# Attention and MLP interleaved on one core: bursts of up to four score chunks between whole FFN2 groups

## The chip, the cores and the metric

The kernel runs on one core of one Trainium2 chip. The metric is the device time of one execution in microseconds (us); less is better. The core has a matrix engine (PE, with PEld for its weight loads), a vector engine (DVE), a scalar engine (ACT), GpSimd (POOL) and a queue engine (SP) that issues DMAs. Matmul results go to PSUM, which has eight banks; DVE and ACT read them from there and write to SBUF.

## The reference

Two layers follow each other. For each of 8 batches and 12 heads, with 448 positions of 64 features:

```
scores = (1/8) * q @ k.T
attn   = max(scores, 0)**2 / 448
out    = attn @ v                       # heads side by side: x, 3584 x 768
h      = x @ w_in                       # 768 -> 2048
g      = max(h, 0) + alpha * min(h, 0)  # alpha per column
result = g @ w_out                      # 2048 -> 768
```

Inputs and output are float32; the kernel multiplies in bf16 and accumulates in float32.

## The kernel before

**Units of work.** Four heads of one batch are a quad; there are 24 quads, three for each batch. A quad has seven score chunks (j = 0 to 6, `scores`, line 150) and one A@V (`attnv`, line 189). A chunk is four matmuls on 64x64 quarters of PE, two for each of two PSUM banks (its halves, r = 0 and 1). Relu turns a chunk in PSUM into a bf16 tile `rl`: with "act" ACT does both halves in one instruction (line 173), with "act2" in two (line 169), with "both" ACT does half 0 and DVE half 1 (lines 165 and 166). `squares` (line 176) then lets DVE square `rl` into `at` (line 184). A@V is 28 quarter matmuls into two banks, which ACT copies, scaled, to `xT` (line 217).

The MLP of a batch is 16 FFN1 steps (`ffn1`, line 224: six matmuls of 448 columns on the whole array into one bank, called hps; ACT makes `neg` at line 238, DVE makes `gT` at line 239) and FFN2 groups (`ffn2`, line 242). A group is 16 matmuls of 384 columns that accumulate in one bank, called ops, and that DVE copies to `osb` (line 255); every second group is followed by two stores on SP. One call of `ffn2` is half a group, 8 matmuls. Batches go in pairs: after the FFN1 of an even batch six groups are ready, after that of an odd batch eight.

**PSUM.** The pool `scps` has two buffers of two banks for chunks and A@V. The pool `mmps` has four buffers of one bank, shared by hps, ops, and by the chunks that are called with `space=mm_ps` (their two halves are two buffers named sch).

**Order.** Everything is written out by hand, and each engine executes its instructions in the order of the program. From batch 1 on, a list `stream` holds the chunks of quads 6 to 23, with the A@V of a quad two chunks into the next quad (line 438). It is cut into bursts of three units after a first one of two (line 441), 49 in all. `spread` (line 314) puts them between the steps of the MLP: in the FFN1 part of a batch two or three, in its FFN2 part five to seven, placed by a share of summed costs, so that a burst may stand between the two halves of a group. In a burst (`group`, line 288) the scores come first and A@V last; of three units, the first chunk uses `mmps`. Then come the squares, and for the chunk with j = 0 the SP work of later quads: `load` of q, k, v of quad n + 2 (line 91), and DMA transposes of k and q of quad n + 1 (line 128). With j = 4, POOL casts q, k and v of quad n + 2 to bf16 (line 109). The DMA queue of SP works in order.

Batch 0 and the first six quads stand in a part of their own ahead of this loop, and the FFN of batch 7 follows after it.

Of the kernel before, what the change touches and what calls it, by code (L numbers as in the profile page):

```python
# [24 lines left out]
def kernel(  # L25
# [10 lines left out]
    nc = tc.nc  # L36
    B, H, S, D = q.shape
    d_model, d_ff = moe_w_in.shape
    assert H * D == d_model and S == PP * NJ and D == 64 and H % 4 == 0
    NG = H // 4  # L40
# [7 lines left out]
    def pool(name, bufs, **kw):  # L48
        return ctx.enter_context(tc.tile_pool(name=name, bufs=bufs, **kw))
# [5 lines left out]
    v_pool = pool("vp", 4)  # L55
    early_pool = pool("early", 2)
    qkT_pool = pool("qkT", 2)
    rl_pool = pool("rl", 3)
    at_pool = pool("at", 10)
    xT_pool = pool("xT", 2)  # L60
    g_pool = pool("g", 2)
    neg_pool = pool("neg", 3)
    o_pool = pool("o", 3)
    sc_ps = pool("scps", 2, **PSUM)
    mm_ps = pool("mmps", 4, **PSUM)
# [39 lines left out]
    def copy(eng, o, i):  # L105
        if eng is nc.scalar:
            nc.scalar.copy(o, i)
        else:
            eng.tensor_copy(o, i)  # L109

    def to_bf16(n, w, eng):
        r = raw.pop((n, w))
        if w == "v":
            t = v_pool.tile([128, 2, NJ, D], BF16, tag="v", name="vb")
            vb[n] = t
            copy(eng, t, r)
        else:
            t = cast_pool.tile([128, NJ, 2, D], BF16, tag=w, name=f"{w}b")
            cast[(n, w)] = t
            copy(eng, t.rearrange("p j s d -> p s j d"), r)  # L120
# [29 lines left out]
    def scores(n, j, relu="act", space=sc_ps):  # L150

        if space is mm_ps:
            half = [mm_ps.tile([128, 512], F32, tag="mm", name="sch") for _ in range(2)]
        else:
            ps = sc_ps.tile([128, 2, 512], F32, tag="sc", name="sc")
            half = [ps[:, r] for r in range(2)]
        for r in range(2):
            for c in range(2):
                nc.tensor.matmul(half[r][64 * c:64 * c + 64, :S],  # L159
                                 kT[n][64 * r:64 * r + 64, j, c, :],  # L160
                                 qT[n][64 * r:64 * r + 64, :, c, :],
                                 start=True, stop=True)
        rl = rl_pool.tile([128, 2, S], BF16, tag="rl", name="rl")
        if relu == "both":
            nc.scalar.activation(rl[:, 0], half[0][:, :S], ACTF.Relu)  # L165
            nc.vector.tensor_scalar(rl[:, 1], half[1][:, :S], 0.0, None, ALU.max)  # L166
        elif relu == "act2":
            for r in range(2):
                nc.scalar.activation(rl[:, r], half[r][:, :S], ACTF.Relu)  # L169
        elif relu == "dve":  # L170
            nc.vector.tensor_scalar(rl, ps[:, :, :S], 0.0, None, ALU.max)
        else:
            nc.scalar.activation(rl, ps[:, :, :S], ACTF.Relu)  # L173
        todo.append((n, j, rl))

    def squares(keep=0, both=False):
        while len(todo) > keep:
            n, j, rl = todo.pop(0)
            a = at_pool.tile([128, 2, S], BF16, tag="at", name="at")
            if both:  # L180
                nc.scalar.activation(a[:, 0], rl[:, 0], ACTF.Square)
                nc.vector.tensor_tensor(a[:, 1], rl[:, 1], rl[:, 1], ALU.mult)
            else:
                nc.vector.tensor_tensor(a, rl, rl, ALU.mult)  # L184
            att[(n, j)] = a
# [38 lines left out]
    def ffn1(b, ff, kms=range(KM)):  # L224
        if b % 2 == 0 and ff == 0 and kms[0] == 0:
            gT[b // 2] = g_pool.tile([128, KF, 2 * S], BF16, tag="g", name="gT")
        if kms[0] == 0:
            hps[ff] = mm_ps.tile([128, S], F32, tag="mm", name="hps")
        ps = hps[ff]
        for km in kms:  # L230
            nc.tensor.matmul(ps, w_in_sb[:, km // 2, km % 2, bass.ts(ff, 128)],  # L231
                             xT[b][:, km // 2, km % 2, :],
                             start=(km == 0), stop=(km == KM - 1))
        if kms[-1] != KM - 1:
            return

        neg = neg_pool.tile([128, S], F32, tag="neg", name="neg")
        nc.scalar.activation(neg, ps, ACTF.Relu, scale=-1.0)  # L238
        nc.vector.scalar_tensor_tensor(gT[b // 2][:, ff, (b % 2) * S:(b % 2) * S + S],  # L239
                                       neg, beta_sb[:, ff:ff + 1], ps, ALU.mult, ALU.add)  # L240

    def ffn2(sb, c, hf, half):
        if half == 0:
            ops[(sb, c, hf)] = mm_ps.tile([128, 384], F32, tag="mm", name="ops")
        ps = ops[(sb, c, hf)]
        for ff in range(8 * half, 8 * half + 8):
            nc.tensor.matmul(ps, gT[sb][:, ff, bass.ts(c, 128)],  # L247
                             w_out_sb[:, ff, bass.ts(hf, 384)],
                             start=(ff == 0), stop=(ff == KF - 1))
        if half == 0:  # L250
            return
        if (sb, c) not in o_sb:
            o_sb[(sb, c)] = o_pool.tile([128, d_model], F32, tag="o", name="osb")
        o = o_sb[(sb, c)]
        nc.vector.tensor_copy(o[:, bass.ts(hf, 384)], ps)  # L255
        if hf == 1:
            for u in range(2):
                blk = 2 * c + u
                b, j = 2 * sb + blk // NJ, blk % NJ
                rows = out[b * S:(b + 1) * S].rearrange("(pp j) d -> j pp d", j=NJ)  # L260
                nc.sync.dma_start(out=rows[j], in_=o[64 * u:64 * u + 64])
# [18 lines left out]
    def steps(b, what):  # L280
        if what == "in":
            return [(1.12, lambda ff=ff: ffn1(b, ff)) for ff in range(KF)]
        cs = range(0, 3) if b % 2 == 0 else range(3, 7)
        return [(1.3, lambda c=c, hf=hf, h=h: ffn2(b // 2, c, hf, h)) for c in cs for hf in range(2) for h in range(2)]


    NQ = len(quads)
    def group(units, how="both"):

        def f():  # L290
            order = sorted(units, key=lambda u: u[1] == "av")
            for i, (n, j) in enumerate(order):
                if j == "av":
                    attnv(n)
                elif i == 0 and len(order) == 3:
                    scores(n, j, how, mm_ps)
                else:
                    scores(n, j)
            squares()
            for n, j in order:  # L300
                if n < n_pe:
                    continue
                if j == 0:
                    if n + 2 < NQ:
                        load(n + 2)
                    if n + 1 < NQ:
                        transpose(n + 1, "k")
                        transpose(n + 1, "q")
                if j == 4 and n > 2 * NG and n + 2 < NQ:
                    for w in "kqv":  # L310
                        to_bf16(n + 2, w, nc.gpsimd)
        return f

    def spread(seq, items, share=0.92):

        total = sum(x[0] for x in seq) * share
        done, n = 0.0, 0
        for cost, fn in seq:
            while n < len(items) and done >= total * n / len(items):
                items[n]()  # L320
                n += 1
            fn()
            done += cost
        assert n == len(items)
# [83 lines left out]
    def g(*units):  # L408
        return group([(int(u[0]), "av" if u[1:] == "a" else int(u[1:])) for u in units])
# [24 lines left out]
    stream = []  # L434
    for n in range(2 * NG, NQ):
        for j in range(NJ):
            stream.append((n, j))
            if j == 1 and n > 2 * NG:
                stream.append((n - 1, "av"))
    stream.append((NQ - 1, "av"))  # L440
    parts = [stream[:2]] + [stream[i:i + 3] for i in range(2, len(stream), 3)]

    count = 0
    for b in range(1, B - 1):
        n_in, n_out = ((2, 7 if b == 1 else 6) if b % 2 else (3, 5))
        if b == B - 2:
            n_out = len(parts) - count - n_in
        mlp = steps(b, "in")
        bursts = [group(x, "act2") for x in parts[count:count + n_in]]
        if b == 1:  # L450
            bursts.append(lambda: [to_bf16(2 * NG + 2, w, nc.gpsimd) for w in "kqv"])
        spread(mlp[3:] if b == 1 else mlp, bursts, 0.95)
        count += n_in
        spread(steps(b, "out"), [group(x) for x in parts[count:count + n_out]], 0.92)
        count += n_out
    for _, fn in steps(B - 1, "in") + steps(B - 1, "out")[:-4]:
        fn()
    ffn2_last(B // 2 - 1, NJ - 1)
# [30 lines left out]
```

## Time and profile before

| what | value |
|---|---|
| median of 8 runs | 398.59 us (397.36 to 399.82) |
| the profiled execution | 398.51 us |
| its span, first to last instruction | 396.7 us |
| granted PE clock, mean | 0.991 |
| DVE busy | 256.3 us (65%) |
| ACT busy | 220.8 us (56%) |
| POOL busy | 70.7 us (18%) |
| PE, FFN1 matmuls (line 231) | 768, 150.7 us |
| PE, FFN2 matmuls (line 247) | 864, 147.9 us |

The span is 1.8 us shorter than the profiled execution's own time; a change of the span is a change of the time. The busy time of PE is built from modelled ends of matmuls that overlap, so what an interval on PE costs is better read from where the rows start. A wait on PE that is shorter than a matmul's modelled length does not show as idle time.

### The profile page before, as it was taken

Reading aid. Unit: us, or ns where it says so; the run is one execution under the profiler, and the core shown is the slowest. Engines: PE = TensorE matmul, PEld = TensorE weight load, DVE = VectorE, ACT = ScalarE, POOL = GpSimd, SP = SyncE. Lnnn points to the kernel's source line nnn. Section 1 sums busy time; section 2 is a strip of 40 time slices with the busy share of each in tenths; the row PEclk is TensorE's granted clock in tenths of the full one; section 3 lists DMA queues with packets and bytes.
Section 4 is the critical chain, followed back from the end, with each engine's and each line's share of the span. In section 5 each row is a group of like instructions: output and inputs, shape, how many; then the busy total and the mean of one; then the engine's idle time right before and its main releaser. Section 6 shows DMA issues by size and latency. Waiting matters only on the chain.

```text
span 396.7 us, 7988 instructions
## 1 busy us (share of the span) xinstructions
PE 386.2 (97%) x3217; PEld 202.2 (51%) x3217; DVE 256.3 (65%) x416; ACT 220.8 (56%) x347; POOL 70.7 (18%) x88
## 2 busy tenths in 40 slices
PE   8788999999999999999999999999999999999996
PEld 5434455445555445544555455554555545555564
DVE  3775866677685767577665787768676676636421
ACT  5785856676465766456544675556454575524300
POOL 6664000022030250032010360033002300000000
PEclk9699999999999999999999999999999999999999
DMA  6999997493498963393088971296048820120033
GB/s 140 187 208 204 204 226 255 96 271 100 102 198 189 215 190 80 85 276 97 2 210 183 244 222 23 67 263 186 2 126 183 224 49 0 41 64 17 0 81 80
DMA packets 64485, 55.45 MB, mean 140 GB/s; under 512 B 35760, under 2 KB 60224, under 8 KB 64448
## 3 DMA queue, kind: packets, MB, share of 16 engines
q1 hardware_dynamic: 53232, 44.78, 44.7%
q0 software_dynamic: 10976, 9.96, 15.8%
q8 instruction: 25, 0.41, 0.4%
q10 hardware_dynamic: 240, 0.20, 0.2%
q14 instruction: 12, 0.10, 0.1%
HBM read 45.62 MB, written 11.01 MB: 143 GB/s over the span
## 4 chain that ended last, share of the span: by engine, by line
PE 91%; DMA 6%; ACT 1%; issue 0%; DVE 0%; ACTq 0%; POOLq 0%
PE ops L247 36%; PE hps L231 36%; PE av L202 7%; PE sc L159 4%; PE sch L159 4%; DMA ke<-in_k_dram 3%; DMA w_in_sb<-in_moe_w_in_dram 2%; DMA vb<-in_v_dram 2%; PE ops L270 1%; PE warm L336 1%; PE tps L134 1%; ACT rl L173 0%; ACT xT L217 0%; DVE osb L272 0%; DVE warm_x L330 0%
## 5 line engine op out<-in xcount | busy, mean ns | idle before, releaser
L231 PE MATMUL hps<-xT,w_in_sb 128*128 128x448 bf16 x768 | 150.7, 353 | 1.3 <-ACT xT L211 0.5
L247 PE MATMUL ops<-w_out_sb,gT 128*128 128x384 bf16 x864 | 147.9, 327 | 0.0
L184 DVE TENSOR_TENSOR at<-rl 128x896 bf16<-128x896 bf16 x167 | 109.7, 678 | 19.7 <-ACT rl L173 8.8
L247 PEld LDWEIGHTS <-gT 128*128 128x128 bf16 x864 | 81.1, 98 | 64.9 <-issue 14.2
L231 PEld LDWEIGHTS <-w_in_sb 128*128 128x128 bf16 x768 | 73.3, 98 | 75.2 <-issue 9.5
L239 DVE SCALAR_TENSOR_TENSOR gT<-neg,beta_sb,hps 128x448 bf16<-128x448 f32 x128 | 84.0, 677 | 36.6 <-ACT neg L238 36.4
L238 ACT ACTIVATE neg<-hps 128x448 f32<-128x448 f32 x128 | 68.5, 553 | 56.8 <-PE hps L231 56.0
L173 ACT ACTIVATE rl<-sc 128x896 bf16<-128x896 f32 x109 | 95.4, 926 | 2.1 <-PE sc L159 1.8
L255 DVE COPY osb<-ops 128x384 f32<-128x384 f32 x54 | 30.0, 555 | 51.5 <-PE ops L247 51.5
L165 ACT ACTIVATE rl<-sch 128x448 bf16<-128x448 f32 x44 | 23.9, 544 | 60.7 <-PE sch L159 60.7
L109 POOL CAST kb<-kraw 128x896 bf16<-128x896 f32 x16 | 15.1, 943 | 210.4 <-DMA kraw<-in_k_dram 210.4
L166 DVE TENSOR_SCALAR rl<-sch 128x448 bf16<-128x448 f32 x44 | 27.3, 621 | 15.2 <-PE sch L159 15.2
L159 PE MATMUL sc<-qT,kT 64*64 64x448 bf16 x440 | 34.3, 360 | 2.9 <-ACT rl L173 2.2
L202 PE MATMUL av<-at,vb 64*64 64x448 bf16 x616 | 33.1, 350 | 0.0
L159 PEld LDWEIGHTS <-kT 64*64 64x64 bf16 x672 | 14.9, 106 | 28.7 <-issue 23.8
L202 PEld LDWEIGHTS <-vb 64*64 64x64 bf16 x672 | 20.3, 110 | 13.3 <-issue 1.4
L217 ACT ACTIVATE xT<-av 128x896 bf16<-128x896 f32 x21 | 19.4, 922 | 7.4 <-PE av L202 7.3
L169 ACT ACTIVATE rl<-sch 128x448 bf16<-128x448 f32 x28 | 13.7, 543 | 16.9 <-PE sch L159 16.9
L159 PE MATMUL sch<-qT,kT 64*64 64x448 bf16 x232 | 22.6, 379 | 0.0
L109 POOL CAST qb<-qraw 128x896 bf16<-128x896 f32 x16 | 17.2, 1078 | 0.0
L109 POOL CAST vb<-vraw 128x896 bf16<-128x896 f32 x16 | 16.7, 1044 | 1.0 <-DMA vraw<-in_v_dram 0.9
L144 POOL DMA_DIRECT2D w_in_sb<-in_moe_w_in_dram x12 | 7.6, 636 | 4.6 <-DMA vb<-in_v_dram 2.1
(52 smaller groups left out, 75.5 us busy)
## 6 DMA issues: line engine op xcount, KB each, us to landing
out_dram<-osb SPq DMA_DIRECT2D x54, 192.0 KB, 2.8
qraw<-in_q_dram SPq DMA_DIRECT2D x19, 448.0 KB, 4.7
kraw<-in_k_dram SPq DMA_DIRECT2D x19, 448.0 KB, 5.3
vraw<-in_v_dram SPq DMA_DIRECT2D x18, 448.0 KB, 6.3
w_out_sb<-in_moe_w_out_dram POOLq DMA_DIRECT2D x2, 1536.0 KB, 20.8
w_in_sb<-in_moe_w_in_dram POOLq DMA_DIRECT2D x8, 192.0 KB, 8.0
w_in_sb<-in_moe_w_in_dram POOLq DMA_DIRECT2D x4, 384.0 KB, 9.7
vb<-in_v_dram POOLq DMA_DIRECT2D x6, 224.0 KB, 10.1
```

The lines of the kernel that those rows point to most:

```text
L109: eng.tensor_copy(o, i)
L159: nc.tensor.matmul(half[r][64 * c:64 * c + 64, :S], kT[n][64 * r:64 * r + 64, j, c, :], qT[n][64 * r:64 * r + 64, :, c, :], start=True, st ...
L165: nc.scalar.activation(rl[:, 0], half[0][:, :S], ACTF.Relu)
L166: nc.vector.tensor_scalar(rl[:, 1], half[1][:, :S], 0.0, None, ALU.max)
L173: nc.scalar.activation(rl, ps[:, :, :S], ACTF.Relu)
L184: nc.vector.tensor_tensor(a, rl, rl, ALU.mult)
L202: nc.tensor.matmul(half[r][64 * s:64 * s + 64, :S], vb[n][64 * r:64 * r + 64, s, j, :], a[64 * r:64 * r + 64, s], start=(j == 0), stop=(j ...
L231: nc.tensor.matmul(ps, w_in_sb[:, km // 2, km % 2, bass.ts(ff, 128)], xT[b][:, km // 2, km % 2, :], start=(km == 0), stop=(km == KM - 1))
L238: nc.scalar.activation(neg, ps, ACTF.Relu, scale=-1.0)
L239: nc.vector.scalar_tensor_tensor(gT[b // 2][:, ff, (b % 2) * S:(b % 2) * S + S], neg, beta_sb[:, ff:ff + 1], ps, ALU.mult, ALU.add)
L247: nc.tensor.matmul(ps, gT[sb][:, ff, bass.ts(c, 128)], w_out_sb[:, ff, bass.ts(hf, 384)], start=(ff == 0), stop=(ff == KF - 1))
L255: nc.vector.tensor_copy(o[:, bass.ts(hf, 384)], ps)
```

## The change

The FFN2 part of a batch is no longer handed to `spread`. It is written as whole groups of two `ffn2` calls, and a table says after which group a burst stands and how many units it takes: after groups 0, 2, 3, 4 and 6 of batch 1; 0, 2, 3, 5 and 6 of the other odd batches; 0, 2, 3 and 4 of the even ones. Bursts have four units in 18 of these places and three or fewer in the others. The FFN1 part keeps bursts of three; batch 1 gets one more there. A@V of a quad now follows after three chunks of the next quad instead of two.

In a burst of four the first chunk is on `mmps` with "act2". A second chunk is on `mmps` too, with "both": the last of four chunks, or the third of three chunks that are followed by A@V. Its two banks are the next two that `mmps` hands out.

The pool `rl` goes from 3 to 5 buffers, `at` from 10 to 14, and `gT` from 2 to 1.

```diff
-    rl_pool = pool("rl", 3)
-    at_pool = pool("at", 10)
+    rl_pool = pool("rl", 5)
+    at_pool = pool("at", 14)
...
-    g_pool = pool("g", 2)
+    g_pool = pool("g", 1)
...
-    def group(units, how="both"):
+    def group(units, how=("both", "both")):
...
+            m = len(order)
+            in_mm = {3: [0], 4: [0, 2 if order[-1][1] == "av" else 3]}.get(m, [])
             for i, (n, j) in enumerate(order):
                 if j == "av":
                     attnv(n)
-                elif i == 0 and len(order) == 3:
-                    scores(n, j, how, mm_ps)
+                elif i in in_mm:
+                    scores(n, j, how[in_mm.index(i)], mm_ps)
                 else:
                     scores(n, j)
...
-            if j == 1 and n > 2 * NG:
+            if j == 2 and n > 2 * NG:
                 stream.append((n - 1, "av"))
...
     for b in range(1, B - 1):
...
+            bursts = [group(take(3), ("act2",)) for _ in range(2 if b % 2 else 3)]
+        spread(mlp, bursts, 0.95)
...
+        if b == 1:
+            sizes = {0: 4, 2: 4, 3: 3, 4: 4, 6: 4}
+        elif b == B - 2:
+            sizes = {0: 4, 2: 4, 3: 3, 4: 1}
+        elif b % 2:
+            sizes = {0: 4, 2: 4, 3: 3, 5: 4, 6: 3}
+        else:
+            sizes = {0: 4, 2: 4, 3: 4, 4: 3}
+        mlp = steps(b, "out")
+        for i in range(0, len(mlp), 2):
+            mlp[i][1]()
+            mlp[i + 1][1]()
+            if i // 2 in sizes:
+                group(take(sizes[i // 2]), ("act2", "both") if sizes[i // 2] == 4 else ("both",))()
```

More of the change, by code (lines that the diff above doesn't have):

```diff
@@ L437, with take @@
             stream.append((n, j))
-            if j == 1 and n > 2 * NG:
+            if j == 2 and n > 2 * NG:
                 stream.append((n - 1, "av"))
     stream.append((NQ - 1, "av"))
-    parts = [stream[:2]] + [stream[i:i + 3] for i in range(2, len(stream), 3)]
-    count = 0
+    def take(m):
+        x = stream[:m]
+        del stream[:m]
+        return x
     for b in range(1, B - 1):
-        n_in, n_out = ((2, 7 if b == 1 else 6) if b % 2 else (3, 5))
-        if b == B - 2:
-            n_out = len(parts) - count - n_in
         mlp = steps(b, "in")
-        bursts = [group(x, "act2") for x in parts[count:count + n_in]]
         if b == 1:
[L451 to L455, printed above, removed]
+            bursts = [group(take(2)), group(take(3), ("act2",)),
+                      lambda: [to_bf16(2 * NG + 2, w, nc.gpsimd) for w in "kqv"], group(take(3), ("act2",))]
+            mlp = mlp[3:]
+        else:
[7 more added lines that the diff above has]
+            sizes = {0: 4, 2: 4, 3: 3, 5: 4, 6: 3}
+        else:
+            sizes = {0: 4, 2: 4, 3: 4, 4: 3}
[5 more added lines that the diff above has]
+                group(take(sizes[i // 2]), ("act2", "both") if sizes[i // 2] == 4 else ("both",))()
+    assert not stream
     for _, fn in steps(B - 1, "in") + steps(B - 1, "out")[:-4]:
```

## The prediction

> **What bounds the kernel now.** First the page: busy times, then the slices.
>
> ```profile
> PE 386.2 (97%) x3217; PEld 202.2 (51%) x3217; DVE 256.3 (65%) x416; ACT 220.8 (56%) x347; POOL 70.7 (18%) x88
> ...
> PE   8788999999999999999999999999999999999996
> ```
>
> PE is the bound, and from the third slice on without a visible hole. The list of waits, for PE alone from 79 us to the end, has one entry:
>
> ```profile
> PE hps L231 <- ACT xT L217: 0.2, 1, 0.2
> ```
>
> So PE's time is its matmuls, the cost of switching between MLP and bursts, and stalls too short to show as idle. Next the timeline, PE around 200 to 213 us, with the other engines' rows of the burst at 208 us (start, length; a row is a run of like instructions):
>
> ```profile
> 203.54 0.38 PE L159 MATMUL sch<-qT,kT 64*64 64x448 bf16 x4
> ...
> 208.08 0.38 PE L159 MATMUL sch<-qT,kT 64*64 64x448 bf16 x4
> 208.18 0.56 DVE L255 COPY osb<-ops 128x384 f32<-128x384 f32 x1 [2.18 <-PE ops L247]
> 208.29 0.55 PE L159 MATMUL sc<-qT,kT 64*64 64x448 bf16 x8
> 208.50 0.54 ACT L165 ACTIVATE rl<-sch 128x448 bf16<-128x448 f32 x1 [2.09 <-PE sch L159]
> 208.66 0.61 DVE L166 TENSOR_SCALAR rl<-sch 128x448 bf16<-128x448 f32 x1
> 208.77 4.07 PE L247 MATMUL ops<-w_out_sb,gT 128*128 128x384 bf16 x24
> ...
> 212.78 0.38 PE L159 MATMUL sch<-qT,kT 64*64 64x448 bf16 x4
> ```
>
> For the pure rates I take the unbroken FFN2 at the end, where a copy follows each group, and an A@V in the chain that ended last:
>
> ```profile
> 375.06 0.56 DVE L255 COPY osb<-ops 128x384 f32<-128x384 f32 x1 [1.34 <-PE ops L247]
> 377.66 0.56 DVE L255 COPY osb<-ops 128x384 f32<-128x384 f32 x1 [2.04 <-PE ops L247]
> ```
> ```profile
> 204.12 1.32 PE av L202 x28
> ```
>
> A group of 16 takes 2.60 us, 0.1625 a matmul. Four quarter matmuls run side by side: 1.32 / 7 = 0.19 us for a set, so a chunk is 0.19 and an A@V 1.32.
>
> **1. Fewer bursts.** From the burst at 208.08 to the next at 212.78 are 4.70 us: 24 x 0.1625 = 3.90 for FFN2, 3 x 0.19 = 0.57 for chunks, and 0.23 left. From 203.54 to 208.08: 4.54 - 2.60 - 2 x 0.19 - 1.32 = 0.24. A burst costs about 0.23 us whatever is in it: the change of PE's tiling, in and out. Chunks, A@V and MLP matmuls stay the same in number. The stream of 144 units made 49 bursts; now there are 43 (8 in batch 1, 7 in each of five others). 6 x 0.23 = **-1.4 us**. Cutting a group in two cost nothing beyond its burst, so whole groups gain nothing more.
>
> The Trainium skill ("TensorEngine Tiling (Array Packing)", Key Properties) says that changing the tiling mode drains the array, and "TensorE: Matmul & The Clock Gate" (Step-by-step: what each phase is for) puts a drain at about 128 cycles; at its 2.4 GHz two drains are an estimated 0.11 us a burst. The row says 0.23; by the page the gain would be 0.6 us instead of 1.4, and the sum below 401.2.
>
> **2. The second chunk on `mmps`.** This is what decides. `mmps` has four buffers. Counted in the program's order, after a group come the two halves of the first chunk, then the two of the second such chunk: the last of these four is the bank of the group just finished. The order of the changed program's instructions shows it: in each of the 18 bursts of four this half waits for DVE's copy of the group in front of the burst. In no burst of this loop before did a chunk need that bank.
>
> From the rows at 208, with the burst's first matmul as zero: the copy starts at 0.10 and ends at 0.66 (208.74). A matmul starts some 0.05 after DVE has freed its bank (below: at 175.11, after the first `gT` since 174.39, of 0.67). So the half may start at 0.71. Without a wait the third chunk would start at 0.21 + 0.19 = 0.40, the fourth at 0.59. PE takes its instructions in order, and what follows waits too.
> - Three chunks and A@V: 0.71 - 0.40 = 0.31 us. There are 7: in batch 1 after groups 0 and 6, in batches 3 and 5 after group 0, in batches 2, 4 and 6 after group 2. 7 x 0.31 = 2.2.
> - Four chunks: 0.12 us. The next group takes the bank of the first chunk's half 0, which ACT frees at 0.42 + 0.54 + 0.05 = 1.01, where it would have started at 0.69 + 0.19 = 0.88; so 0.13 in all. 11 x 0.13 = 1.4.
>
> Sum **+3.6 us**. Bounds: nothing, if the wait is hidden in some way that the rows do not show (it can't be a gain: a wait only delays). Above: the copy can start late, if DVE is behind. It is tight where one group alone lies between a burst and one of four: after group 3 of batches 2 and 4, and after group 4 of batch 1. In the first two the burst before (three chunks and A@V) gives DVE a half relu, done about 1.7 us after the burst's start, and three squares of 0.62: 3.6. The next copy is due at 1.83 (from 203.54 to the next `ops` at 205.37) + 0.19 + 0.31 + 2.60 + 0.2 = 5.1. Batch 1 has about as much to spare. Squares can take twice as long next to POOL's casts:
>
> ```profile
> 171.79 0.93 POOL L109 CAST kb<-kraw 128x896 bf16<-128x896 f32 x1 [22.68 <-DMA kraw<-in_k_dram]
> 171.91 2.55 DVE L184 TENSOR_TENSOR at<-rl 128x896 bf16<-128x896 bf16 x2 [0.18 <-ACT rl L173]
> 174.39 2.44 DVE L239 SCALAR_TENSOR_TENSOR gT<-neg,beta_sb,hps 128x448 bf16<-128x448 f32 x4
> 175.11 1.99 PEld L231 LDWEIGHTS <-w_in_sb 128*128 128x128 bf16 x11 [0.28 <-issue]
> ```
>
> Two squares take 2.55 instead of 1.24. Three so slowed add 1.9, which would make the copy some 0.4 to 0.6 late: at three places up to 1.8 us. I take the undisturbed rows, as those casts fall elsewhere.
>
> **3. Two old stalls.** In the rows above FFN1 waits at 175.11 for a bank (0.19 us), as at 316.27 (0.12): squares slowed by casts, right behind a burst. In the changed order the casts there start about as the burst does, and not 2 us into it; the squares are through in time. **-0.3 us**; between -0.3 and, were each stall doubled, +0.3.
>
> **4. What is covered.** In a burst of four with one group behind it, DVE has 0.56 + 0.61 + 4 x 0.62 = 3.65 us and ACT 2 x 0.54 + 2 x 0.93 + 0.54 = 3.5, against 0.1 + 0.88 + 0.13 + 2.60 = 3.7 on PE: the last square waits for ACT's last relu, so the next copy is some 0.45 late, but there a burst of three follows, which does not need that bank. `rl` and `at` only get more buffers; ACT waited 0.3 us once for an `rl`, off PE's path. With one `gT`, the first write of a pair must follow the last read of the pair before; PE has ended that read before it starts the FFN1 step whose result is written, so the wait is over when it is asked: 0.
>
> SP and POOL keep their sequence; what moves is time. A transpose is late when stores and loads stand ahead of it:
>
> ```profile
> 199.18 1.13 SPq L261 DMA_DIRECT2D out_dram<-osb  x2
> 200.37 0.58 SPq L91 DMA_DIRECT2D qraw<-in_q_dram  x1
> 203.61 3.73 SPq L128 DMA_TRANSPOSE qT<-qb  x1
> ```
>
> This `qT` landed at 210.90, 10.5 us after that load's start (in the trace's other such cases 10.5 to 11.2), and was used at 212.78. In batches 3 and 5 of the changed order the same chain runs from the end of group 1: 0.75 for the copy, 1.2 for the stores (199.18 to 200.37), 10.5 to 11.2: landed after 12.5 to 13.2. Its first use is the fourth chunk behind group 5, after four groups (10.4), a burst of four (1.1), one of two chunks and A@V (1.9) and 0.7: 14.1. Covered, with 0.9 to 1.6 us to spare; if that is gone, PE stands still for what is missing, at two places.
>
> **Sum.** 398.5 - 1.4 + 3.6 - 0.3 = **400.4 us**, against this execution's 398.51; the median of the runs is 398.59.
>
> **Rivals.**
> - *The waits do not bite* (0.12): faster. The only loss is the 18 waits, so they decide: the sign turns where their mean falls under 1.7 / 18 = 0.09 us. If the copy ended before the half is due, the result is 398.5 - 1.7 = 396.8. For it: nothing in the profile; against it: the copy begins only 0.10 after the burst and takes 0.56 every time.
> - *Half of it* (0.18): only the A@V bursts pay, and in the others the wait sinks into the change of tiling behind the fourth chunk: 398.5 - 1.7 + 2.2 = 399.0. For it: 0.13 is small against a row; against it: the change of tiling comes after the late half.
> - *DVE or the transposes fall behind* (0.15): 400.4 + 1.8 for three late copies, or + 0.5 to 1 for each late transpose: 401.3 to 402.2.
> - The forecast itself (0.55): 399.9 to 401.0, with the prices of 0.31 and 0.13 give or take 0.03 (18 x 0.03 = 0.5), and step 3 up to its upper end.
>
> A measurement of this kernel tells about 0.3% (1.2 us) from no change. Slower by more: the third, and the forecast but for 0.05 that the spread of the runs takes below 399.7: 0.65. Same: those 0.05, the second, and 0.02 of the first, 0.25. Faster: 0.10. The range leaves out the first rival and the top of the third: 398.2 to 401.9.
>
> **What would show it.** The trace after should have 43 bursts; in each of the 18 of four, the last sch half should start 0.71 us after the burst's first matmul, 0.05 after the copy's end; the chain should pass through `osb` at line 255; the waits at 175 and 316 should be gone. Wrong if that half starts at 0.40 or 0.59, if bursts cost other than 0.23, or if a transpose ends a wait of PE.

## The result, and the profile after

| | before | after |
|---|---|---|
| median | 398.45 us (32 runs, 397.11 to 399.82) | 400.29 us (11 runs, 399.42 to 401.02) |
| the profiled execution | 398.51 us | 400.25 us |
| its span | 396.7 us | 398.5 us |
| time of after / time of before | | 1.0048 [1.0035, 1.0061] |

The change makes the kernel 1.8 us slower, half a per cent. Ratios, here and below, leave out runs more than 1.5% above the fastest of their kernel (two runs of experiment 3); the medians are of all runs. First the page of after: busy times and the chain of work that ended last, by engine.

```profile
PE 387.7 (97%) x3217; PEld 205.1 (51%) x3217; DVE 251.5 (63%) x409; ACT 223.4 (56%) x366; POOL 72.4 (18%) x88
...
PE 90%; DVE 3%; ACT 2%; DMA 2%; issue 1%; POOL 0%; ACTq 0%
```

PE does the same 3217 matmuls and is as full as before. The list of PE's waits from 79 us on is empty: by that view alone nothing is lost. The loss is in the timeline, in waits shorter than a matmul's modelled length. This is after, PE, DVE and ACT around a burst of three chunks and A@V (start, length, engine, line):

```profile
192.83 0.38 PE L159 MATMUL sch<-qT,kT 64*64 64x448 bf16 x4
192.93 0.56 DVE L255 COPY osb<-ops 128x384 f32<-128x384 f32 x1 [1.34 <-PE ops L247]
193.04 0.36 PE L159 MATMUL sc<-qT,kT 64*64 64x448 bf16 x4
193.23 0.69 PE L159 MATMUL sch<-qT,kT 64*64 64x448 bf16 x4
...
193.55 1.69 PE L202 MATMUL av<-at,vb 64*64 64x448 bf16 x28
...
195.18 0.50 PE L247 MATMUL ops<-w_out_sb,gT 128*128 128x384 bf16 x2
```

The first chunk takes 0.38 us as a row, the third 0.69: 0.31 more with the same four matmuls. The copy of the group in front ends at 193.49 (192.93 + 0.56); the third chunk's second half, the late half from here on, starts at 193.55, and A@V right behind it. The same view eight microseconds later, a burst of four chunks:

```profile
200.48 0.38 PE L159 MATMUL sch<-qT,kT 64*64 64x448 bf16 x4
200.59 0.56 DVE L255 COPY osb<-ops 128x384 f32<-128x384 f32 x1 [2.04 <-PE ops L247]
200.70 0.55 PE L159 MATMUL sc<-qT,kT 64*64 64x448 bf16 x8
200.90 0.98 ACT L169 ACTIVATE rl<-sch 128x448 bf16<-128x448 f32 x2 [4.62 <-PE sch L159]
...
201.07 0.50 PE L159 MATMUL sch<-qT,kT 64*64 64x448 bf16 x4
...
201.51 0.66 PE L247 MATMUL ops<-w_out_sb,gT 128*128 128x384 bf16 x3
```

Here the last chunk is 0.50 long, 0.12 more. Taken from the starts of single matmuls, the late half (here that of the last chunk) starts 0.717 to 0.720 us after the burst's first matmul in every one of the 18 bursts of four, 0.05 after the copy's end. Where a burst costs 0.19 for each set of four matmuls and 0.22 besides, the 25 others leave no rest at all (0.00 each); the seven with A@V leave 0.334 each, the eleven of four chunks 0.144: 2.34 + 1.59 = 3.93 us.

**Two parts of the program.** From the first burst of the loop (at about 79 us) to the last matmul of the program, before took 312.87 us in its profile and after 315.61: 2.74 more, where the spans differ by 1.8. The rest is ahead of the loop, in instructions that are the same. In before's one profile the first burst comes at 80.17, in after's at 79.16. The granted PE clock, on the page of before and then on that of after:

```profile
PEclk9699999999999999999999999999999999999999
```
```profile
PEclk9899999999999999999999999999999999999999
```

The second slice is 0.6 in before and 0.8 in after. So before's own execution came to the loop 1.0 us late, after a lower clock. That the clock is the cause is likely, not shown: of the 46 runs of before beside the experiments, the 12 with a granted clock of 0.991 or less, as in this profile, have a median of 398.8 us, the 13 with 0.998 or more 397.8; but experiment 1's profile, with 0.9 in that slice, is no earlier at the loop than after's.

### The profile page after: what moved, and what is told of

Same layout as the page of the kernel before. It is cut to its first block, busy times and chain, and to the rows that moved or that the text cites. A ratio compares the mean times of both kernels' runs of the same rounds, so it can differ in the third digit from the quotient of the medians.

```text
span 398.5 us, 7955 instructions
## 1 busy us (share of the span) xinstructions
PE 387.7 (97%) x3217; PEld 205.1 (51%) x3217; DVE 251.5 (63%) x409; ACT 223.4 (56%) x366; POOL 72.4 (18%) x88
## 4 chain that ended last, share of the span: by engine, by line
PE 90%; DVE 3%; ACT 2%; DMA 2%; issue 1%; POOL 0%; ACTq 0%
PE ops L247 36%; PE hps L231 34%; PE av L202 7%; PE sch L159 6%; PE sc L159 4%; DVE at L184 2%; DMA qe<-in_q_dram 2%; PE ops L270 1%; ACT rl L173 1%; PE tps L134 1%; DMA qraw<-in_q_dram 1%; PE avh L202 1%; DVE gT L239 0%; ACT rl L169 0%; ACT neg L238 0%
## 5 line engine op out<-in xcount | busy, mean ns | idle before, releaser
L173 ACT ACTIVATE rl<-sc 128x896 bf16<-128x896 f32 x97 | 85.1, 930 | 1.8 <-PE sc L159 1.8
L169 ACT ACTIVATE rl<-sch 128x448 bf16<-128x448 f32 x66 | 32.3, 542 | 67.1 <-PE sch L159 67.1
L202 PE MATMUL av<-at,vb 64*64 64x448 bf16 x616 | 34.5, 350 | 0.0
L159 PE MATMUL sc<-qT,kT 64*64 64x448 bf16 x392 | 30.5, 356 | 3.3 <-ACT rl L173 2.2
L159 PEld LDWEIGHTS <-kT 64*64 64x64 bf16 x672 | 17.0, 105 | 32.2 <-issue 26.2
L159 PE MATMUL sch<-qT,kT 64*64 64x448 bf16 x280 | 30.5, 370 | 0.0
L165 ACT ACTIVATE rl<-sch 128x448 bf16<-128x448 f32 x37 | 20.7, 560 | 13.5 <-PE sch L159 13.5
L166 DVE TENSOR_SCALAR rl<-sch 128x448 bf16<-128x448 f32 x37 | 22.9, 620 | 8.4 <-PE sch L159 8.4
L202 PEld LDWEIGHTS <-vb 64*64 64x64 bf16 x672 | 21.4, 109 | 11.7 <-issue 1.4
L109 POOL CAST vb<-vraw 128x896 bf16<-128x896 f32 x16 | 18.0, 1126 | 0.0
```

Source lines behind the costliest of these rows:

```text
L159: nc.tensor.matmul(half[r][64 * c:64 * c + 64, :S], kT[n][64 * r:64 * r + 64, j, c, :], qT[n][64 * r:64 * r + 64, :, c, :], start=True, st ...
L202: nc.tensor.matmul(half[r][64 * s:64 * s + 64, :S], vb[n][64 * r:64 * r + 64, s, j, :], a[64 * r:64 * r + 64, s], start=(j == 0), stop=(j ...
```

## The experiments

Each ratio is against the kernel before on the same chip (its medians there: 398.29 us for experiments 1 to 4, 398.14 for 5 to 7).

**1. The pools alone.** Before, with the three new buffer counts.

```diff
-    rl_pool = pool("rl", 3)
-    at_pool = pool("at", 10)
-    g_pool = pool("g", 2)
+    rl_pool = pool("rl", 5)
+    at_pool = pool("at", 14)
+    g_pool = pool("g", 1)
```

> The kernel before with the buffer counts of the changed one alone (rl 5, at 14, gT 1); order and bursts as before. My theory (bursts gain 1.4 us, the wait for the copy of the group just finished loses 3.9): the pools do nothing, 398.5 us, a ratio of 1.000, and the loop has the same two stalls of FFN1. Rival (the pools do part of it: the changed kernel's profile reached its first burst of the loop 1.0 us earlier than before's): about 397.4, with that burst near 79.2 us in place of 80.2. Second rival (one gT buffer makes DVE wait between pairs of batches): slower than 398.5, with a wait of PE at the start of batches 2, 4 and 6.

398.42 us, ratio 1.0008 [0.9993, 1.0023]: the pools do nothing. With before's order of work, its profile has the loop's first burst at 79.13, so before's 1.0 us there isn't the order's. Its loop takes 313.68, because FFN1 waits five times for a bank, 0.11 to 0.44 us, 1.15 in all, where before's profile had two waits, 0.31 in all. So such waits differ between two profiles with one and the same order of work; whether the buffer counts have a part in that, one profile of each does not tell.

**2. The late half after A@V.** The changed kernel, with A@V ahead of the third chunk in the seven bursts that have both.

```diff
-            in_mm = {3: [0], 4: [0, 2 if order[-1][1] == "av" else 3]}.get(m, [])
+            av_last = order[-1][1] == "av"
+            in_mm = {3: [0], 4: [0, 3]}.get(m, [])
+            if m == 4 and av_last:
+                order = order[:2] + [order[3], order[2]]
```

> The changed kernel with one swap: in the seven bursts of three chunks and A@V, A@V (1.32 us) goes ahead of the third chunk, so that the bank of the group just finished is asked for at 0.40 + 1.32 = 1.7 us after the burst's start, with the copy done at 0.66. Nothing else changes, 43 bursts. My theory: 7 x 0.33 = 2.3 us less, 398.0 us; the eleven bursts of four chunks keep their 0.14. Rival (a second chunk on the shared banks costs by itself, wherever it stands): no change, 400.3.

397.52 us, ratio 0.9987 [0.9972, 1.0002]; after stood at 1.0048, so this edit gives back 0.6%, 2.4 us. Timeline of this kernel, the same burst as above:

```profile
191.22 0.38 PE L159 MATMUL sch<-qT,kT 64*64 64x448 bf16 x4
191.32 0.56 DVE L255 COPY osb<-ops 128x384 f32<-128x384 f32 x1 [1.34 <-PE ops L247]
191.43 0.36 PE L159 MATMUL sc<-qT,kT 64*64 64x448 bf16 x4
...
191.62 1.49 PE L202 MATMUL av<-at,vb 64*64 64x448 bf16 x28
...
192.94 0.36 PE L159 MATMUL sch<-qT,kT 64*64 64x448 bf16 x4
...
193.24 0.34 PE L247 MATMUL ops<-w_out_sb,gT 128*128 128x384 bf16 x1
```

The copy starts 0.10 and ends 0.66 after the burst's start as before, but nobody waits for it: the third chunk comes at 1.72, and takes 0.36. These seven bursts lose 0.01 us together instead of 2.34, with the chunk still on `mmps`: a second chunk there costs nothing by itself. The eleven of four chunks, which have no A@V to put ahead, still lose 0.144 each. The loops of the two profiles differ by 2.73: 2.33 from the seven bursts, and 0.40 because FFN1 waits 0.11 us for a bank here and 0.51 in after.

**3. Bursts of three or fewer.** The changed kernel's whole groups, but 50 bursts, none of four, one after nearly every group.

```diff
-            sizes = {0: 4, 2: 4, 3: 3, 5: 4, 6: 3}
+            sizes = {0: 3, 1: 3, 2: 3, 3: 3, 4: 3, 5: 3, 6: 3}
...
-            sizes = {0: 4, 2: 4, 3: 4, 4: 3}
+            sizes = {0: 3, 1: 3, 2: 3, 3: 3, 4: 3}
```

> The changed kernel with whole groups and all its buffers, but bursts of at most three units: 50 of them, 7 more than in the changed kernel and one more than before, and no second chunk on the shared banks. My theory: 7 x 0.22 = 1.5 us more for bursts, 3.9 us less for the waits: 400.3 - 2.4 = 397.9; measured against before one burst more, 398.5 + 0.2 = 398.7 (the two sums differ by what the profiles' first 80 us differ, 1.0 us, and by 0.2 in FFN1's stalls). Rival (whole groups themselves cost, since all the copies now come right at a burst): 400 or more. Second rival (whole groups gain by themselves): below 397.5.

409.73 us (six runs, 404.91 to 412.94), ratio 1.0244 [1.0202, 1.0286]: about 10 us slower by the ratio, and not the test it was meant to be. The list of PE's waits (total, times, longest) has an entry that neither before nor after has:

```profile
PE sc L159 <- DMA qT<-qb: 7.4, 2, 4.1
```

Timeline of SP's queue and of PE at the first of the two:

```profile
154.49 1.12 SPq L261 DMA_DIRECT2D out_dram<-osb  x2
156.06 0.40 SPq L91 DMA_DIRECT2D qraw<-in_q_dram  x1
...
157.61 1.97 SPq L128 DMA_TRANSPOSE kT<-kb  x1
159.68 3.23 SPq L128 DMA_TRANSPOSE qT<-qb  x1
```
```profile
161.94 0.36 PE L159 MATMUL sc<-qT,kT 64*64 64x448 bf16 x4
165.62 0.38 PE L159 MATMUL sc<-qT,kT 64*64 64x448 bf16 x4 [3.32 <-DMA qT<-qb]
165.93 4.45 PE L247 MATMUL ops<-w_out_sb,gT 128*128 128x384 bf16 x16
```

The transpose stands behind stores, loads and another transpose; its first user starts 11.1 us after the first of them, but the denser bursts ask for it earlier. The stalls cost twice: the group behind the first took 4.38 us (165.93 to 170.31), that behind the second 5.01, against 2.70 elsewhere with its change of tiling, because PE's granted clock fell to 0.83 from 160 to 170 us and 0.66 from 260 to 270. Priced by starts, the two bursts lose 3.5 and 4.5 us and the groups behind them 1.7 and 2.3; with one burst more than before (0.22) that is 12.2 of the 12.3 us by which the loop of this profile is longer than that of before's.

**4. Three chunks in each burst.** 43 bursts, three chunks each but the last; A@V goes into FFN2 bursts ahead of the third chunk, so that the late half always has A@V in front of it. Batch 1 begins with a burst of three instead of two.

```diff
+    def burst(av=False):
+        x = chunks[:3]
+        del chunks[:3]
+        return x + ([(turned.pop(0), "av")] if av else [])
...
+            plan = {0: True, 2: True, 3: False, 4: True}
...
+                units = [(turned.pop(0), "av")] if av is None else burst(av)
+                group(units, ("act2", "both") if av else ("both",))()
```

> A version that keeps the 43 bursts and drops the waits: every burst has three chunks, and three bursts of a batch have A@V besides, all of them in the FFN2 part, with A@V ahead of the third chunk, which alone uses a second pair of the shared banks. My theory: the six bursts less give 1.3 us, no wait is left, FFN1's stalls stay 0.3 to 0.5: 398.5 - 1.3 = 397.2, from 396.8 to 397.6; faster than both. Rival (a second chunk on the shared banks costs by itself; 16 remain): 397.2 + 16 x 0.2 = 400.4. Second rival (fewer bursts gain nothing): 398.5.

396.77 us, ratio 0.9965 [0.9948, 0.9983]: below both kernels. All 18 waits are gone: none of the 17 late halves here has one. A new one of 0.65 us stands at the loop's first burst. Timeline of PE there:

```profile
79.02 0.38 PE L159 MATMUL sch<-qT,kT 64*64 64x448 bf16 x2
...
79.68 0.38 PE L159 MATMUL sch<-qT,kT 64*64 64x448 bf16 x2 [0.28 <-DVE gT L239]
```

A chunk on `mmps` there needs a bank of an FFN1 result that DVE has not yet turned into `gT`; the chunk's second half starts 0.66 after the first.

**5. The copy twice.** After, with a second DVE copy of the group (into a scratch tile) ahead of each of the 18 bursts, to see whether the late half follows the copy's end.

```diff
+        if twice and twice.pop():
+            nc.vector.tensor_copy(scratch, ps)
         nc.vector.tensor_copy(o[:, bass.ts(hf, 384)], ps)
```

> The changed kernel with the suspected wait made longer: DVE copies the group ahead of each of the 18 bursts of four twice, first to a spare tile, then to its output. The second copy ends some 0.48 us later (DVE starts its next instruction 0.48 after the copy at 208 us in the kernel before). My theory: the late half starts at 1.19 in place of 0.72 in all 18, 18 x 0.48 = 8.6 us more, 408.9 us. Rival (the late half is held by something else, so that the copy has slack): up to 0.5 us more, 400.8.

405.16 us, ratio 1.0165 [1.0136, 1.0195]: neither number. Timeline of this kernel at a burst of four chunks:

```profile
106.33 0.38 PE L159 MATMUL sch<-qT,kT 64*64 64x448 bf16 x4
...
106.44 0.56 DVE L259 COPY scratch<-ops 128x384 f32<-128x384 f32 x1 [2.04 <-PE ops L250]
...
106.75 0.98 ACT L169 ACTIVATE rl<-sch 128x448 bf16<-128x448 f32 x2 [4.70 <-PE sch L159]
...
106.91 0.55 DVE L260 COPY osb<-ops 128x384 f32<-128x384 f32 x1
106.92 0.80 PE L159 MATMUL sch<-qT,kT 64*64 64x448 bf16 x4
```

Its list of PE's waits names the releaser:

```profile
PE sch L159 <- ACT rl L169: 1.8, 7, 0.3
```

The second copy ends at 107.46 (106.91 + 0.55). The late half starts at 107.35, before that: 106.75 + 0.54 for the first of ACT's two relus + 0.05. With the extra reader the pool gave the half another bank, that of the burst's own first chunk, and it waits for ACT instead. The waits in bursts grow from 3.93 to 9.25. So the half waits for the last reader of whatever bank it is given. In the eleven bursts of four chunks the next group starts 0.309 us behind the late half, here (1.013 to 1.322) as in after (0.718 to 1.027): it follows the late half. The experiment does not say what a copy of twice the length would cost in after's own assignment.

**6. Bursts of three or fewer, placed for the transposes.** As 3, but with the extra burst in the FFN1 part of even batches, and free places behind groups 2 or 3.

```diff
-            bursts = [group(take(3), ("act2",)) for _ in range(2 if b % 2 else 3)]
+            bursts = [group(take(3), ("act2",)) for _ in range(2 if b % 2 else 4)]
...
-            sizes = {0: 4, 2: 4, 3: 3, 5: 4, 6: 3}
+            sizes = {0: 3, 1: 3, 2: 3, 4: 3, 5: 3, 6: 3}
...
-            sizes = {0: 4, 2: 4, 3: 4, 4: 3}
+            sizes = {0: 3, 1: 3, 3: 3, 4: 3}
```

> The bursts of three between whole groups once more, 50 of them, with the burst that starts a quad moved: in batches 2, 4 and 6 a fourth burst in the FFN1 part, the others after groups 0, 1, 3 and 4, so that the transposes for the next quad are issued where no store stands ahead of them on SP. My theory (bursts 0.22 each, whole groups free, e3's loss was two late transposes): no wait of PE for a DMA, one burst more than before, 398.3 + 0.2 = 398.5, ratio 1.000 to 1.002. Rival (whole groups cost): slower by more than 1 us with no DMA wait. Rival (whole groups gain): below 397.5.

398.87 us, ratio 1.0010 [0.9994, 1.0027]; no wait for a DMA. Whole groups with bursts of three in them are worth nothing by themselves: one burst more than before (0.22), 0.95 of waits for `gT` in FFN1 bursts, and 0.5 at one `ops`, in place of before's 0.31 in FFN1, make 1.4 of the 1.5 us by which its loop is longer than in before's profile.

**7. The two leftovers of 4.** Batch 1 begins with a burst of two again (one burst of four chunks makes up for it), and in batches 2 to 6 POOL holds the casts of the first FFN1 burst until that burst's last square, by a copy of one element of each partition, which reads that square.

```diff
+                    if held:
+                        nc.gpsimd.tensor_copy(hold, att[order[-1]][:, 0, 0:1])
                     for w in "kqv":
                         to_bf16(n + 2, w, nc.gpsimd)
...
+        bursts = [group(burst(m=2))] if b == 1 else []
```

> The version of 43 bursts without waits (e4) with two of its blemishes taken away. First, batch 1 starts with a burst of two chunks as in all other kernels (e4's of three waited 0.65 us there) and has one of four after group 2 (0.14). Second, in batches 2 to 6 POOL's casts that belong to the first burst of the FFN1 part wait for that burst's squares. My theory (squares are slowed only while POOL casts beside them, and FFN1 stalls where the last two are): the squares of those five bursts take 0.62 us each and FFN1 has no stall behind them, while bursts that are not held can still have both; 0.5 to 0.9 us faster than e4, 396.1. Rival (the slow squares come from the DMAs that land then): they stay at 1.1 to 1.35. Second rival (held casts make a transpose late): a wait of PE for kT or qT, slower than e4.

396.39 us, ratio 0.9944 [0.9924, 0.9964]: the best of all, 2.2 us below before by the ratio and 1.8 by the medians. First the timeline of experiment 4, POOL and DVE behind the first FFN1 burst of batch 2, then that of 7 at the same place:

```profile
127.73 0.93 POOL L109 CAST kb<-kraw 128x896 bf16<-128x896 f32 x1 [11.60 <-DMA kraw<-in_k_dram]
127.83 2.58 DVE L184 TENSOR_TENSOR at<-rl 128x896 bf16<-128x896 bf16 x2 [0.19 <-ACT rl L173]
...
128.61 1.32 POOL L109 CAST qb<-qraw 128x896 bf16<-128x896 f32 x1
```
```profile
126.60 0.63 DVE L184 TENSOR_TENSOR at<-rl 128x896 bf16<-128x896 bf16 x1 [0.77 <-ACT rl L169]
127.41 0.62 DVE L184 TENSOR_TENSOR at<-rl 128x896 bf16<-128x896 bf16 x1 [0.18 <-ACT rl L173]
...
128.22 0.63 DVE L184 TENSOR_TENSOR at<-rl 128x896 bf16<-128x896 bf16 x1 [0.19 <-ACT rl L173]
...
128.91 0.19 POOL L319 COPY hold<-at 128x1 bf16<-128x1 bf16 x1 [13.78 <-DVE at L184]
129.03 0.93 POOL L109 CAST kb<-kraw 128x896 bf16<-128x896 f32 x1
```

Two squares beside casts take 2.58 us, held apart 0.62 to 0.63 each; so it is in all five held bursts. FFN1's waits for a bank, 0.57 us in experiment 4's profile, are gone, and so is the 0.65; the one burst of four chunks costs 0.146. That is -1.07, and the loops of the two profiles differ by -1.06. Of the 0.57, only 0.22 (at 131.05) stood behind a burst that is now held. The other three waits stood behind bursts that are not held; their casts now come 0.6 to 1.6 us later in the burst, but that they are gone for this reason is not shown. The step from 4 to 7 is inside the spread of their ratios, so it rests on the traces.

## Why the prediction was right, and where not

It named 400.4 us and the side, slower; the median is 400.29. The mechanism is the forecast's, a late half that waits for the copy of the group just finished; that the sum comes out so closely is luck, because errors cancel.

- **Step 1, fewer bursts: right.** There are 43, and a burst costs 0.22 us besides its matmuls, so -1.32 instead of -1.4. The estimate of 0.11 us a burst, from the drain that the Trainium skill states ("TensorE: Matmul & The Clock Gate", Step-by-step: what each phase is for), is half of what the rows show; the measurement decides.
- **Step 2, the late half: right, a little too small.** The half starts at 0.72 (forecast 0.71), 0.05 after the copy's end; 0.334 and 0.144 a burst instead of 0.31 and 0.13, so 3.93 instead of 3.6. What was not counted is some 0.02 in each: the half's start, 0.01 later, and the start of what stands behind it. Experiment 2 shows this as the cause of the A@V bursts: with the order of two units exchanged, 2.3 of the 2.34 us are gone, and the time falls by 2.4. For the eleven others the forecast's reason was another: the next group at 1.01, when ACT frees its bank, and so 0.13. It starts at 1.03, 0.31 behind the late half, and experiment 5 shows the same 0.31 with the late half moved to 1.01. So the late half holds it, and not ACT; that 0.13 came near 0.144 is luck in this.
- **Step 3, the old stalls: wrong.** "In the changed order the casts there start about as the burst does [...] the squares are through in time", -0.3. The places at 175 and 316 are free, but after has two new stalls in FFN1, 0.26 us at 131.54 and 0.25 at 139.39. At the first of these the casts start 0.92 us behind the burst's first matmul, and all three of its squares lie beside them. Timeline of after, then its chain of waits, which does show this one:

```profile
126.95 0.93 POOL L109 CAST kb<-kraw 128x896 bf16<-128x896 f32 x1 [11.57 <-DMA kraw<-in_k_dram]
...
127.46 3.44 DVE L184 TENSOR_TENSOR at<-rl 128x896 bf16<-128x896 bf16 x3 [0.76 <-ACT rl L169]
127.82 1.33 POOL L109 CAST qb<-qraw 128x896 bf16<-128x896 f32 x1
...
129.09 1.32 POOL L109 CAST vb<-vraw 128x896 bf16<-128x896 f32 x1
```
```profile
126.10 0.37 PE sch L159 x4
...
127.46 3.44 DVE at L184 x3
130.89 0.60 DVE gT L239
131.49 0.04 issue
131.54 2.44 PE hps L231 x12
```

Three squares take 3.44 instead of 1.87, so `gT` is late, and FFN1 gets its bank at 131.49. Against before's profile the step was worth +0.2, against experiment 1, the same order of work, -0.64. It should have been a range of about one microsecond.
- **Step 4, what is covered: right.** No copy in front of a burst of four starts late (0.11 in all 18), no wait of PE ends with a DMA, and the two tight transposes landed 1.50 and 1.55 us ahead of use, at the upper end of the forecast 0.9 to 1.6. Experiment 1 shows that the pools cost nothing, experiment 3 what it costs when that cover is gone: 3.5 and 4.5 us at two transposes, and the clock behind it.
- **The sum.** -1.32 + 3.93 + 0.2 = +2.8, and the loops of the two profiles differ by 2.74. The forecast's +1.9 fell 0.9 short of that: 0.1 in step 1, 0.3 in step 2, 0.5 in step 3. The spans differ by 1.8 all the same, because before's profile lost 1.0 us ahead of the loop; the forecast stood on that execution without noticing it. Against experiment 1, which has no such loss, it is -1.32 + 3.93 - 0.64 = +1.97, and its loop is 1.93 shorter than after's; the medians differ by 1.84. There, step 3 gained 0.34 more than forecast and hid what the other two fell short.
- **The rivals.** "The waits do not bite" falls with the rows; "half of it" falls with the eleven bursts, which pay 0.144 each in after and in experiment 2 alike. Late copies and transposes did not occur in after.
- **What would show it.** Not seen: the chain does not pass through `osb`. These waits are too short to look like idle time, so neither the chain nor the list of waits names them; only the starts do.

## What to carry to other kernels

A second pair of banks from a shared pool can be the bank whose reader has just begun: find it by counting the pool's buffers in program order, and put long work that needs no bank of it (here A@V, 1.32 us) between the reader and the matmul that needs it. On a full engine, waits of 0.1 to 0.3 us do not show as idle time: set a cost for each kind of burst from rows of starts, and what is left over is the wait. One profile of before is one draw: compare its stages with a second profile of the same order before small differences are put into a sum, and check the lead of every transfer when bursts are moved.

## What the runs showed of the hardware

- Squares of two SBUF inputs (0.62 us alone) and POOL's casts (0.93 alone) slow each other: three squares in 3.44 us beside casts of 1.32. By their starts there is one of each about every 1.27 (127.82 to 129.09), where alone in a row a square starts every 0.54 and a cast every 0.87, 1.41 together. The Trainium skill ("SBUF — State Buffer", Who interferes with whom) says that a DVE instruction with two SBUF inputs contends with a GpSimd instruction that reads SBUF, and calls the ports that they share an exclusive lock; these rows agree that the two contend, but a pair takes less than one after the other.
- After PE had stood still for 3.3 and 4.1 us, the next group took 4.38 and 5.01 us instead of 2.70 (experiment 3). The Trainium skill ("TensorE: Matmul & The Clock Gate", What's actually happening) puts the return to half clock after at least one idle window of about 3.4 us; two stalls of about that length and more are in keeping with it, but no run here shows where the threshold lies.
- One more reader of a tile changed which bank the pool gave to a later one (experiment 5), so an added instruction is not a clean way to lengthen a wait.
